# Attention and two MLPs on one core: pairing TensorE's work by width, splitting weights from the decoded tile, and planning the DMAs

## The chip, the cores and the metric

The kernel runs on one core of one Trainium2 chip. The metric is the device time of one execution in microseconds (us). Three runs of the kernel before have a median of 832.0 us (830.35 to 835.03).

## The reference

Inputs and outputs are fp32. Batch 2, 8 heads, 768 positions, head size 64; 16 clusters per head.

```python
mask = argmax(q_n @ c_n) == argmax(k_n @ c_n)      # same cluster
attn = softmax(where(mask, q @ k.T / 8, -1e9)) @ v   # -> x [1536, 512]
h = x @ w_in                                         # 512 -> 2048
x = (h * sigmoid(1.702 * h)) @ w_out                 # 2048 -> 512
out = (silu(x @ w_gate) * (x @ w_val)) @ w_out2      # 512 -> 1536 -> 512
```

The weights of both MLPs arrive in HBM as 64-bit numbers, since setup multiplies them by a 64-bit factor. The kernel decodes them on chip.

## The kernel before, in words

**Attention** comes first (to about 260 us), in an order written out by hand. Beside it the first ten weight items are decoded. The change does not touch this part.

**Precision.** A product of fp32 numbers is made of three TensorE passes over a high and a low part (`product`, L347 on): high by high, high by low, low by high. Each operand is therefore split: `high` is a cast on ScalarE (ACT, L343), `low` a subtraction on VectorE (DVE, L346).

**Decoding.** An item is half of a weight key: 128 partitions by 512 numbers, 512 KB as it arrives ("raw") and 256 KB decoded. The keys are `1`, `2` (first MLP, eight each) and `g`, `v`, `3` (second MLP, six each). `plan_decode` (L940) plans for each item: a DMA of raw into one of three buffers (L242), two ACT operations `small` and `low_bits` (L257, L260), two DVE operations `joined` and `signed` (L263, L268), and a DMA that stores the result in a DRAM scratch (`keep`, L272 on; the second halves of `1`, `g` and `v` take two DMAs). Later `plan_fetch` (L952) reads a whole key back from the scratch (512 KB, L340) into `w`, each time that a batch needs it.

**Units.** The rest is a list of 28 units: for the first MLP two batches of eight, for the second two batches of six. A unit covers 256 hidden columns of 768 rows. Its first stage (`s1`) multiplies x by the unit's weights with moving tiles 384 wide; the trace calls the result `h`. The first batch's units of the first MLP ("classic") have 8 steps of six matmuls; the others use a seven-product scheme (`plan_products`, L1043), once in the first MLP and twice (gate and value) in the second. The activation goes to `c`, is split into `g`, and the second stage (`s2`, the tiles `a` of the trace) multiplies `g` by the split weights `sp` and accumulates in six PSUM banks: `plan_m1_s2` (L1125) for the first MLP in groups of three matmuls, 512 and 256 wide by turns, `plan_m2_s2` (L1191) for the second in groups 512 wide.

**Order.** The loop at the end (L1341 on) goes over the units k = 0 to 27: it plans decodes, splits the second-stage weights of unit k+1, prepares the first-stage weights of unit k+3, and lays the first stage of unit k+2 beside the second stage of unit k: `beside_each_other` (L1291) takes a step of one and a step of the other by turns. This fixes TensorE's order. A decode's ACT operations may not start before the last TensorE task planned when the decode was created (`after`); its raw DMA may.

**The planner.** `Plan.order` (L91) is a list scheduler. It gives each task a latest start, counted back from TensorE's nominal times, then simulates the engines with the tasks' costs and `AFTER` (L64: the time from a task's end to a follower on another engine), and emits each engine's instructions in the order found. On the chip each engine, and SyncE (SP), which issues the DMAs, works in that order. A DMA task occupies SP for 80 ns (160 for a store) in this simulation, and its follower is free 3000 ns later. How many items are decoded, and when, is set by `AHEAD` and `DECODES` (L195): four before the first unit, then five per unit in the classic batch, one per unit in the first MLP's second batch, three per unit after that, in the one order of `items`.

Of the kernel before, what the change touches and what calls it, by code (L numbers as in the profile page):

```python
# [21 lines left out]
class Task:  # L22


    def __init__(self, engine, ns, emit, deps):
        self.engine, self.ns, self.emit, self.deps = engine, ns, emit, set(deps)
        self.end = self.latest = None
# [28 lines left out]
class Plan:  # L56
# [6 lines left out]

    AFTER = {"PE": 230.0, "ACT": 160.0, "DVE": 150.0, "POOL": 120.0, "SP": 3000.0}  # L64

# [25 lines left out]
    def order(self, pe_start, free):  # L91
        for r in self.rings:
            for k, h in enumerate(r.held):
                if h.first is None:
                    continue
                for t in h.users:
                    if k >= r.n:
                        t.deps.update(r.held[k - r.n].users)
                    if k and r.held[k - 1].first is not None:
                        t.deps.add(r.held[k - 1].first)  # L100
        pe = [t for t in self.tasks if t.engine == "PE"]
        for a, b in zip(pe, pe[1:]):
            b.deps.add(a)
        nexts = {t: [] for t in self.tasks}
        left = {t: len(t.deps) for t in self.tasks}
        for t in self.tasks:
            for d in t.deps:
                nexts[d].append(t)
# [9 lines left out]
        def gap(t, s):  # L118
            return 0.0 if t.engine == s.engine == "PE" else self.AFTER[t.engine]

# [9 lines left out]
        left = {t: len(t.deps) for t in self.tasks}  # L130
        ready = {e: [] for e in self.AFTER}
# [5 lines left out]
        while len(done) < len(self.tasks):  # L137
# [31 lines left out]
            for s in nexts[t]:  # L169
                left[s] -= 1  # L170
                if not left[s]:
                    r = max((d.end + gap(d, s) for d in s.deps), default=0.0)
                    ready[s.engine].append((r, s))
# [6 lines left out]
def tile_cluster_attention_two_mlps(ctx: ExitStack, tc: tile.TileContext, qk, v, cen, w1, w2, wg, wv, w3, out):  # L180
# [10 lines left out]
    NB = 512  # L191
    scale = 1.0 / float(D) ** 0.5
    NQK = 5
    RAW, WB, EB, CB, GB, XC, X0 = 3, 3, 2, 4, 4, 7, 4
    DECODES, AHEAD = (5, 1, 3), 4  # L195

# [89 lines left out]

    def new_w():
        return wo_p.tile([128, 512], F32, tag="wo", name="wo")

    def take_in():  # L290

        while True:
            it = items[started[0]]
            fetch_to(started[0] + 1)
            started[0] += 1
            raw = raw_t.pop(it)
            a, t = new_a(), new_t()
            small(a, raw)
            low_bits(t, raw)
            fetch_to(started[0] + 2)  # L300
            joined(t, a)
            yield
            w = new_w()
            signed(w, a, t)
            keep(it, w)
            yield
# [576 lines left out]
    def late(name):  # L883
        if not late_pools:
            att.close()
            xf_p.append(pool(ctx, "xf1", 1))
            xc_p.append(pool(ctx, "xc1", XC - X0))
            xs_p.append(pool(ctx, "xs", 2))
            b_p.extend(pool(ctx, f"b{i}", 1) for i in (1, 2))
            late_pools.update(  # L890
                s=pool(ctx, "s", 1), e=pool(ctx, "e", EB), g=pool(ctx, "g", GB), sp=pool(ctx, "sp", 3),
                a=pool(ctx, "ps_a", 1, space=PSUM),
            )
        return late_pools.get(name)
# [13 lines left out]
    def after_late(make):  # L908
# [6 lines left out]
        "raw": p.ring(RAW, new_raw, [Held(r) for r in raw_t.values()]),  # L915
        "a": p.ring(2, new_a), "t": p.ring(2, new_t), "wo": p.ring(2, new_w),
        "w": p.ring(WB, new_wf, w_held),
# [15 lines left out]
    for i in range(6):  # L933
        rings[f"acc{i}"] = p.ring(1, late_tile("a", [128, 512], F32, f"a{i}"))
    late_rings = ["s", "b1", "b2", "g", "sp", "xs", "xc", "xf", "p1", "u2", "u3"] + [f"acc{i}" for i in range(6)]

    raw_held = dict(zip(raw_t, rings["raw"].held))
    kept = {}

    def plan_decode(it, after=()):  # L940
        raw = raw_held.get(it)
        if raw is None:
            raw = rings["raw"].new()
            p.task("SP", 80, lambda: fetch_into(raw.tile, it), (), [(raw, 0)])
        a, t, w = (rings[n].new() for n in ("a", "t", "wo"))
        p.task("ACT", act(570), lambda: small(a.tile, raw.tile), [(raw, 0)], [(a, 0)], after)
        p.task("ACT", act(560), lambda: low_bits(t.tile, raw.tile), [(raw, 0)], [(t, 0)], after)
        p.task("DVE", dve(512), lambda: joined(t.tile, a.tile), [(a, 0)], [(t, 0)])
        p.task("DVE", dve(512), lambda: signed(w.tile, a.tile, t.tile), [(a, 0), (t, 0)], [(w, 0)])
        kept[it] = p.task("SP", 160, lambda: keep(it, w.tile), [(w, 0)])  # L950

    def plan_fetch(key):  # L952
        w = rings["w"].new()
        p.task("SP", 80, lambda: fetch_w(w.tile, key), (), [(w, 0)], [kept[key + (i,)] for i in range(2) if key + (i,) in kept])
        return w
# [9 lines left out]
    def every(n=None):  # L965
        return (slice(None),) if n is None else (slice(None), slice(*n))

    def plan_classic_blocks(key, early):
        if early:
            out = rings["b0"].held[:2]  # L970
            return out
        w, out = plan_fetch(key), []
        for i in range(2):
            out.append(rings["b0"].new())
            plan_high_low(out[-1], every((0, 2)), lambda i=i: w.tile[:, 2 * i:2 * i + 2], [(w, 0)], 0, 512)
        return out
# [23 lines left out]
    def plan_split(key):  # L1000
        w, out = plan_fetch(key), []
        for i in range(2):
            t = rings["sp"].new()
            plan_high_low(
                t, every(), lambda i=i: w.tile[:, 2 * i:2 * i + 2].rearrange("p a c -> p (a c)"), [(w, 0)], 0, 512
            )
            out.append(t)
        return out
# [17 lines left out]
    def plan_classic(blocks, x, c, by_half):  # L1026
        c += [rings["c"].new() for _ in range(2)]
        for f, t in [(f, t) for t in range(2) for f in range(2)] if by_half else [(f, t) for f in range(2) for t in range(2)]:
            ps = rings[f"m{flip[0]}"].new()
            flip[0] ^= 1  # L1030
            for k in range(2):
                pe_block(ps, 0, blocks[f], k if f == 0 else 1 - k, x[k, t], k == 0, k == 1)
                if k == 0:
# [91 lines left out]
    def plan_m1_s2(gs, sp, acc, first, last):  # L1125
        for f, o in [(f, o) for o in range(KC) for f in range(2)] if last else [(f, o) for f in range(2) for o in range(KC)]:
            m = slice(o * 128, (o + 1) * 128)
            c0 = 256 * (o % 2)
            for a, t0, n, at, opens in (
                (acc[o], 0, NB, slice(0, NB), True),  # L1130
                (acc[4 + o // 2], NB, S - NB, slice(c0, c0 + 256), o % 2 == 0),
            ):
                def emit(a=a, t0=t0, n=n, at=at, opens=opens, f=f, m=m):
                    g, w = gs[f].tile, sp[f].tile
                    product(
                        a.tile[:, at], (w[:, 0, m], w[:, 1, m]), (g[:, 0, t0:t0 + n], g[:, 1, t0:t0 + n]),
                        first and f == 0 and opens, last and f == 1,
                    )
                p.task("PE", 3 * mm(n), emit, [(h, (0, i)) for h in (gs[f], sp[f]) for i in range(2)], [(a, o)])
                yield  # L1140

# [49 lines left out]
    def plan_m2_s2(gs, sp, acc, first, last):  # L1191
        for f, o in [(f, o) for o in range(SC) for f in range(2)] if last else [(f, o) for f in range(2) for o in range(SC)]:
# [7 lines left out]
            p.task("PE", 3 * mm(DM), emit, [(h, (0, i)) for h in (gs[f], sp[f]) for i in range(2)], [(acc[o], 0)])  # L1200
            yield

    def plan_m2_out(b, acc):
        for o in range(SC):
# [13 lines left out]
            p.task("DVE" if o % 2 else "ACT", (dve if o % 2 else act)(DM), emit, [(acc[o], 0)], [(osb, 0)])  # L1218
            p.task("SP", 80, send, [(osb, 0)])

# [16 lines left out]

    def decoded(n=0, upto=None):
        after = [t for t in p.tasks if t.engine == "PE"][-1:]
        while todo and (n > 0 or upto in todo):  # L1240
            plan_decode(todo.pop(0), after)
            n -= 1

    def needs(key):
        if key + (1,) in todo:
            decoded(upto=key + (1,))

    def prepare(u):
        kind, b, q = u
        names = ("1", "gv")[kind == "2"]  # L1250
        if u != units[0]:
            for n in names:
# [5 lines left out]
    def split(u):  # L1258
        kind, b, q = u
        n = {"1": "2", "2": "3"}[kind]  # L1260
        needs((n, q))
        split_of[u] = plan_split((n, q))
# [52 lines left out]

    decoded(AHEAD)
    prepare(units[0])
    prepare(units[1])
    beside_each_other(s1(units[0]), products_of(units[0]), last_values(), SC)
    end_of_pv = [t for t in p.tasks if t.engine == "PE"]  # L1320
# [14 lines left out]
    split(units[0])  # L1335
    decoded(DECODES[0])
    prepare(units[2])
# [73 lines left out]
```

## Time and profile before

| What | Value |
|---|---|
| Median of three runs | 832.0 us (830.35 to 835.03) |
| The profiled execution's own time | 832.42 us |
| Its span in the trace | 830.6 us |
| TensorE busy in the span | 809.4 us (97%) |
| VectorE, ScalarE busy | 637.6 us (77%), 473.6 us (57%) |
| DMA traffic | 103.3 MB, mean 124 GB/s |

In the rows below PE is TensorE's matmuls, PEld its weight loads, DVE VectorE, ACT ScalarE, SP SyncE. "SPq" marks an instruction of SP's sequencer, such as the issue of a DMA. L351 is the line of all matmuls of the MLPs, so the tiles tell them apart. Times are counted from the start of the span.

### The profile page before, as it was taken

The page shows a single profiled execution, that of the slowest core. Times are in us where ns is not written, and L with a number is a line of the kernel's source. Part 1 is how long each engine was busy: PE and PEld are TensorE (multiplying, and loading weights), DVE is VectorE, ACT ScalarE, POOL GpSimd, SP SyncE. Part 2 cuts the span into 40 slices and gives each one's busy share as a digit, 9 for nine tenths or more (in the row PEclk, how much of TensorE's full clock was granted, in tenths as well). Part 3 has the DMA queues.
Part 4 walks back from the last instruction along what each step waited for, and adds up shares of the span by engine and source line. Part 5 has one row for each costly group of instructions (what it writes and reads, how often), then busy time and mean ns, then how long its engine had stood idle before and what let it go on. Part 6 is the DMA issues. An engine that isn't in the chain of part 4 may idle for free.

```text
span 830.6 us, 12798 instructions
## 1 busy us (share of the span) xinstructions
PE 809.4 (97%) x4832; PEld 758.4 (91%) x4832; DVE 637.6 (77%) x1164; ACT 473.6 (57%) x818; POOL 36.4 (4%) x48
## 2 busy tenths in 40 slices
PE   8999999999999999898799999999999999999998
PEld 6999999999999998797689999999999999999996
DVE  7888898898873775567889767988877898877752
ACT  7847767766666765666676446645334554343321
POOL 8530000000000000000000000000000000000000
PEclk9999999999999999999999999999999999999999
DMA  6123123121335687778787432321222112321202
GB/s 129 29 82 88 47 68 89 48 67 50 97 123 202 209 301 271 277 248 296 236 301 236 152 116 89 114 90 64 89 77 77 51 52 102 115 89 51 76 1 77
DMA packets 48710, 103.31 MB, mean 124 GB/s; under 512 B 17044, under 2 KB 22248, under 8 KB 48648
## 3 DMA queue, kind: packets, MB, share of 16 engines
q1 hardware_dynamic: 48568, 102.30, 37.8%
q8 instruction: 38, 0.62, 0.3%
q10 hardware_dynamic: 80, 0.20, 0.1%
q14 instruction: 24, 0.20, 0.1%
HBM read 80.77 MB, written 20.97 MB: 122 GB/s over the span
## 4 chain that ended last, share of the span: by engine, by line
PE 79%; DMA 8%; DVE 7%; ACT 4%; issue 1%; SPq 0%; ACTq 0%; DVEq 0%
PE h L351 30%; PE a L351 21%; PE pv L663 14%; PE st L647 8%; PE smax L600 4%; DMA raw<-in_w 4%; DMA raw<-in_wv 2%; DMA raw<-in_wg 2%; DVE nm L605 1%; PE sims L516 1%; ACT a L257 1%; DVE b L346 1%; DMA w<-scr 1%; DVE t L263 1%; ACT t L260 1%
## 5 line engine op out<-in xcount | busy, mean ns | idle before, releaser
L351 PE MATMUL h<-xc,b 128*128 128x384 f32 x1728 | 350.6, 340 | 12.5 <-ACT c L1038 11.7
L351 PEld LDWEIGHTS h<-xc,b 128*128 128x128 f32 x1728 | 307.6, 189 | 36.4 <-ACT c L1038 16.4
L351 PE MATMUL a<-g,sp 128*128 128x512 f32 (+1 forms) x768 | 157.3, 339 | 0.9 <-DVE xf L1154 0.9
L663 PEld LDWEIGHTS pv<-v,p 128*128 128x128 f32 x1152 | 135.5, 192 | 0.1
L663 PE MATMUL pv<-v,p 128*128 128x65 f32 x1152 | 134.9, 273 | 0.0
L351 PEld LDWEIGHTS a<-g,sp 128*128 128x128 f32 x768 | 122.5, 190 | 10.3 <-DVE xf L1154 1.3
L351 PE MATMUL a<-sp,g 128*128 128x512 f32 x432 | 119.7, 394 | 0.0
L654 ACT ACTIVATE p<-st 128x384 f32<-128x384 f32 x192 | 90.3, 491 | 32.7 <-PE st L647 27.4
L605 DVE TENSOR_REDUCE nm<-smax 128x1 f32<-128x384 f32 x192 | 99.9, 556 | 8.4 <-PE smax L600 7.4
L647 PE MATMUL st<-q,k 128*128 128x384 f32 (+1 forms) x384 | 98.3, 347 | 0.1
L351 PEld LDWEIGHTS a<-sp,g 128*128 128x128 f32 x432 | 79.2, 188 | 7.8
L263 DVE SCALAR_TENSOR_TENSOR t<-a,t 128x512 int32<-128x512 int32 x68 | 46.6, 688 | 50.0 <-ACT t L260 49.8
L343 ACT CAST b<-s 128x512 fp32r<-128x512 f32 x64 | 39.5, 617 | 70.7 <-PE h L351 65.1
L257 ACT ACTIVATE a<-raw 128x512 f32<-128x512 f32 x68 | 45.8, 673 | 57.5 <-DMA raw<-in_w 33.1
L343 ACT CAST b<-w 128x768 fp32r<-128x768 f32 (+1 forms) x48 | 36.5, 763 | 71.8 <-PE h L351 65.4
L647 PEld LDWEIGHTS st<-q,k 128*128 128x128 f32 (+1 forms) x384 | 67.5, 190 | 4.4 <-ACT p L654 2.8
L600 PE MATMUL smax<-k,q 80*128 80x384 f32 x192 | 62.8, 344 | 0.5 <-ACT q L576 0.2
L346 DVE TENSOR_TENSOR g<-c,g 128x768 fp32r<-128x768 f32 x56 | 53.0, 952 | 1.3 <-ACT g L343 1.2
L1060 DVE TENSOR_TENSOR u<-h,p 128x384 f32<-128x384 f32 x64 | 35.6, 556 | 21.5 <-PE h L351 21.4
L346 DVE TENSOR_TENSOR b<-w,b 128x768 fp32r<-128x768 f32 (+1 forms) x48 | 41.5, 866 | 10.9 <-ACT b L343 10.7
L268 DVE SCALAR_TENSOR_TENSOR wo<-a,t 128x512 int32<-128x512 int32 x68 | 46.6, 688 | 2.9 <-DMA scr<-wo 1.5
L343 ACT CAST g<-c 128x768 fp32r<-128x768 f32 x56 | 45.9, 839 | 4.8 <-DVE c L1075 4.8
(118 smaller groups left out, 746.0 us busy)
## 6 DMA issues: line engine op xcount, KB each, us to landing
raw<-in_w SPq DMA_DIRECT2D x44, 512.0 KB, 4.9
w<-scr SPq DMA_DIRECT2D x44, 512.0 KB, 4.2
scr<-wo SPq DMA_DIRECT2D x36, 256.0 KB, 2.5
raw<-in_wg SPq DMA_DIRECT2D x12, 512.0 KB, 3.2
raw<-in_wv SPq DMA_DIRECT2D x12, 512.0 KB
w<-scrg SPq DMA_DIRECT2D x12, 512.0 KB
w<-scrv SPq DMA_DIRECT2D x12, 512.0 KB, 3.2
st<-in_qk SPq DMA_DIRECT2D x15, 384.0 KB, 3.9
```

The lines of the kernel that those rows point to most:

```text
L257: nc.scalar.activation(a, raw[:, :, 1].bitcast(F32), ACTF.Copy, scale=2.0**-112)
L263: nc.vector.scalar_tensor_tensor(out=t, in0=a.bitcast(I32), scalar=3, in1=t, op0=ALU.logical_shift_left, op1=ALU.bitwise_or)
L268: nc.vector.scalar_tensor_tensor(out=w.bitcast(I32), in0=a.bitcast(I32), scalar=-(2**31), in1=t, op0=ALU.bitwise_and, op1=ALU.bitwise_or)
L343: nc.scalar.copy(to, of)
L346: eng.tensor_tensor(out=to, in0=of, in1=hi.bitcast(F32), op=ALU.subtract)
L351: nc.tensor.matmul(out=out_ps, lhsT=lhs[a], rhs=rhs[b], start=(start and j == 0), stop=(stop and j == 2), skip_group_check=True, **kw)
L600: nc.tensor.matmul(out=ps, lhsT=q2(h)[0:ONE + NC, 1, c * 128:(c + 1) * 128], rhs=k2(h)[0:ONE + NC, 1, n * HALF:(n + 1) * HALF],)
L605: nc.vector.tensor_reduce(out=nm_t[h][:, c, n:n + 1], in_=ps, axis=AX.X, op=ALU.max)
L647: nc.tensor.matmul(out=ps, lhsT=k2(h)[0:rows, a, c * 128:(c + 1) * 128], rhs=q2(h)[0:rows, a, at], start=(a == 0), stop=(a == 1),)
L654: nc.scalar.activation(p_t[h, c][:, at], ps, ACTF.Exp, scale=scale)
L663: nc.tensor.matmul(out=pv_t[h][:, i, :], lhsT=p[:, i * 128:(i + 1) * 128], rhs=v_t[h % 3][:, c, :], start=(c == 0 and i == 0), stop=(c == ...
L1060: lambda: nc.vector.tensor_tensor(out=to.tile[:, part], in0=ps.tile[:, 0:HALF], in1=other.tile, op=ALU.add),
```

## The change

Four things are changed together. First, the steps of the first stage are taken two at a time (`by_two`), and the second-stage groups too: two 512-wide groups, then two 256-wide ones in the first MLP, two 512-wide ones in the second. Second, in the first batch the weights of `1` and `2` that are not yet decoded are decoded by the unit that needs them into a tile `wd` (four buffers) and split from there; the store to the scratch stays, for the second batch, and the fetch goes. Third, `g`, `v` and `3` are decoded by a quota for each unit, after that unit's own needs; the decodes ahead of the first unit go. Fourth, the planner gives a raw load or a fetch 2000 ns of SP and a store 1000, has other values in `AFTER`, and treats the order within a ring of buffers as an order of starts (`behind`) and no longer of ends.

```diff
-    AFTER = {"PE": 230.0, "ACT": 160.0, "DVE": 150.0, "POOL": 120.0, "SP": 3000.0}
+    AFTER = {"PE": 210.0, "ACT": 80.0, "DVE": 70.0, "POOL": 120.0, "SP": 2200.0}
...
-                    if k and r.held[k - 1].first is not None:
-                        t.deps.add(r.held[k - 1].first)
+                    if k and r.held[k - 1].first is not None and r.held[k - 1].first not in t.deps:
+                        t.behind.add(r.held[k - 1].first)
...
         def gap(t, s):
-            return 0.0 if t.engine == s.engine == "PE" else self.AFTER[t.engine]
+            if t in s.behind:
+                return -t.ns
+            return 0.0 if t.engine == s.engine != "SP" else self.AFTER[t.engine]
...
-    DECODES, AHEAD = (5, 1, 3), 4
+    DECODES = (1, 1, 1, 2, 2, 4, 4, 4) + (2,) * 8 + (1,) * 3
...
-    def plan_decode(it, after=()):
+    def plan_decode(it, after=(), to="wo"):
...
-            p.task("SP", 80, lambda: fetch_into(raw.tile, it), (), [(raw, 0)])
-        a, t, w = (rings[n].new() for n in ("a", "t", "wo"))
+            p.task("SP", 2000, lambda: fetch_into(raw.tile, it), (), [(raw, 0)])
+        a, t, w = (rings[n].new() for n in ("a", "t", to))
...
-        kept[it] = p.task("SP", 160, lambda: keep(it, w.tile), [(w, 0)])
+        kept[it] = p.task("SP", 1000, lambda: keep(it, w.tile), [(w, 0)])
+        return w
...
+    def plan_pair(key):
+
+        if key + (0,) in kept or key + (0,) not in todo:
+            needs(key)
+            w = plan_fetch(key)
+            return [(w, lambda i=i: w.tile[:, 2 * i:2 * i + 2]) for i in range(2)], key[0] == "1"
+        out = []
+        for i in range(2):
+            todo.remove(key + (i,))
+            w = plan_decode(key + (i,), now(), "wd")
+            out.append((w, lambda w=w: w.tile.rearrange("p (a c) -> p a c", a=2)))
+        return out, False
...
     def plan_split(key):
-        w, out = plan_fetch(key), []
-        for i in range(2):
+        out = []
+        for w, view in plan_pair(key)[0]:
...
-        for f, o in [(f, o) for o in range(KC) for f in range(2)] if last else [(f, o) for f in range(2) for o in range(KC)]:
...
+        order = [(f, o) for o in range(KC) for f in range(2)] if last else [(f, o) for f in range(2) for o in range(KC)]
+        for i in range(0, len(order), 2):
+            for t0, n in acc_parts:
+                for f, o in order[i:i + 2]:
...
+    def decoded(n):
+        for it in [it for it in todo if it[0] in "gv3"][:n]:
+            todo.remove(it)
+            plan_decode(it, now())
...
     def products_of(u):
-        return 8 if classic(u) else 7 if u[0] == "1" else 14
+        return 4 if u[0] == "1" else 7
 
     def groups_of(u):
-        return 16 if u[0] == "1" else 12
+        return 4 if u[0] == "1" else 6
+
+    def by_two(products):
+        for _ in products:
+            next(products, None)
+            yield
...
-    decoded(AHEAD)
...
     for k, u in enumerate(units):
-        decoded(DECODES[0 if classic(u) else 1 if u[0] == "1" else 2])
         if k + 1 < n:
             split(units[k + 1])
         if k + 3 < n:
             prepare(units[k + 3])
+        decoded(DECODES[k] if k < len(DECODES) else 0)
         if k + 1 < n:
             gates(units[k + 1])
         if k + 2 < n:
-            beside_each_other(s1(units[k + 2]), products_of(units[k + 2]), s2(u), groups_of(u))
+            beside_each_other(by_two(s1(units[k + 2])), products_of(units[k + 2]), s2(u), groups_of(u))
```

## Rows read from the trace of the kernel before

**Rows 1.** The page: busy time by engine; GB/s moved in 40 slices of the span.
```profile
PE 809.4 (97%) x4832; PEld 758.4 (91%) x4832; DVE 637.6 (77%) x1164; ACT 473.6 (57%) x818; POOL 36.4 (4%) x48
...
GB/s 129 29 82 88 47 68 89 48 67 50 97 123 202 209 301 271 277 248 296 236 301 236 152 116 89 114 90 64 89 77 77 51 52 102 115 89 51 76 1 77
```

**Rows 2.** Four stretches: us, each engine's busy us (count), granted clock, DMA share, GB/s.
```profile
284.00:443.00 159.00, 145.81 (x795) 132.16 (x793) 114.47 (x180) 105.64 (x188) 0.00 (x0) 0.98 0.80 276
443.00:550.00 107.00, 106.99 (x609) 100.25 (x610) 85.88 (x144) 59.15 (x98) 0.00 (x0) 1.00 0.39 131
550.00:716.00 166.00, 166.00 (x874) 154.96 (x873) 138.40 (x249) 75.57 (x122) 0.00 (x0) 1.00 0.21 70
716.00:831.00 115.00, 110.30 (x557) 100.26 (x556) 75.80 (x134) 40.09 (x67) 0.00 (x0) 1.00 0.19 69
```

**Rows 3.** Waits from 284 to 443 us: who for whom, total us, times, longest.
```profile
ACT a L257 <- DMA raw<-in_w: 29.2, 11, 4.6
PEld h L351 <- ACT c L1038: 16.4, 11, 5.1
PE h L351 <- ACT c L1038: 11.7, 7, 4.6
ACT a L257 <- DMA raw<-in_wg: 9.2, 5, 2.7
```

**Rows 4.** Timeline around the longest wait: start, us, instruction, and idle before it.
```profile
396.96 0.42 SPq L242 DMA_DIRECT2D raw<-in_w  x1
...
403.04 0.66 ACT L257 ACTIVATE a<-raw 128x512 f32<-128x512 f32 x1 [4.57 <-DMA raw<-in_w]
...
403.61 0.48 ACT L1038 ACTIVATE c<-h 128x384 f32<-128x384 f32 x1
...
404.14 1.98 PE L351 MATMUL h<-xc,b 128*128 128x384 f32 x6 [4.65 <-ACT c L1038]
```

**Rows 5.** DMA from 284 to 443 us: total, then issues by line, KB each, us to landing.
```profile
DMA packets 16705, 43.90 MB, mean 276 GB/s; under 512 B 1854, under 2 KB 4670, under 8 KB 16693
...
raw<-in_w SPq DMA_DIRECT2D x24, 512.0 KB, 4.8
w<-scr SPq DMA_DIRECT2D x17, 512.0 KB, 5.9
```

**Rows 6.** Ten-microsecond stretches of the same kind as rows 2.
```profile
290.00:300.00 10.00, 10.00 (x59) 9.38 (x58) 8.78 (x13) 7.21 (x14) 0.00 (x0) 1.00 0.97 316
...
330.00:340.00 10.00, 7.92 (x46) 7.12 (x45) 6.10 (x9) 4.88 (x9) 0.00 (x0) 1.00 0.73 247
...
350.00:360.00 10.00, 10.00 (x50) 9.32 (x49) 5.91 (x9) 5.37 (x10) 0.00 (x0) 0.83 0.74 268
...
400.00:410.00 10.00, 5.86 (x25) 5.45 (x26) 7.38 (x12) 6.33 (x11) 0.00 (x0) 0.83 0.64 233
```

**Rows 7.** The chain that ended last: start, us, what; three stretches.
```profile
295.02 1.06 PE h L351 x6
...
297.13 1.06 PE h L351 x6
...
589.99 2.10 PE h L351 x12
592.09 0.70 PE a L351 x3
592.79 1.06 PE h L351 x6
...
810.14 16.38 PE a L351 x72
```

**Rows 8.** Groups of instructions from 284 to 443 us: count, busy us, mean ns, idle before.
```profile
L257 ACT ACTIVATE a<-raw 128x512 f32<-128x512 f32 x44 | 29.6, 673 | 49.3 <-DMA raw<-in_w 29.2 <-DMA raw<-in_wg 9.2 <-DMA raw<-in_wv 7.0
L263 DVE SCALAR_TENSOR_TENSOR t<-a,t 128x512 int32<-128x512 int32 x43 | 29.4, 688 | 30.2 <-ACT t L260 30.1
...
L343 ACT CAST sp<-w 128x512 fp32r<-128x512 f32 x16 | 10.0, 622 | 0.0
```

More of the change, by code (lines that the diff above doesn't have):

```diff
@@ L25, in __init__ @@
     def __init__(self, engine, ns, emit, deps):
-        self.engine, self.ns, self.emit, self.deps = engine, ns, emit, set(deps)
+        self.engine, self.ns, self.emit, self.deps, self.behind = engine, ns, emit, set(deps), set()
         self.end = self.latest = None
@@ L104, in order @@
         nexts = {t: [] for t in self.tasks}
-        left = {t: len(t.deps) for t in self.tasks}
         for t in self.tasks:
-            for d in t.deps:
+            t.behind -= t.deps
+        left = {t: len(t.deps) + len(t.behind) for t in self.tasks}
+        for t in self.tasks:
+            for d in (*t.deps, *t.behind):
                 nexts[d].append(t)
@@ L129, in order @@
                 t.latest = nominal[t]
-        left = {t: len(t.deps) for t in self.tasks}
+        left = {t: len(t.deps) + len(t.behind) for t in self.tasks}
         ready = {e: [] for e in self.AFTER}
@@ L171, in order @@
                 if not left[s]:
-                    r = max((d.end + gap(d, s) for d in s.deps), default=0.0)
+                    r = max((d.end + gap(d, s) for d in (*s.deps, *s.behind)), default=0.0)
                     ready[s.engine].append((r, s))
@@ L915, in tile_cluster_attention_two_mlps @@
         "raw": p.ring(RAW, new_raw, [Held(r) for r in raw_t.values()]),
[L916 removed]
+        "a": p.ring(2, new_a), "t": p.ring(2, new_t), "wo": p.ring(2, new_wo), "wd": p.ring(WO, late_tile("wd", [128, 512], F32, "wd")),
         "w": p.ring(WB, new_wf, w_held),
@@ L934, in tile_cluster_attention_two_mlps @@
         rings[f"acc{i}"] = p.ring(1, late_tile("a", [128, 512], F32, f"a{i}"))
-    late_rings = ["s", "b1", "b2", "g", "sp", "xs", "xc", "xf", "p1", "u2", "u3"] + [f"acc{i}" for i in range(6)]
+    late_rings = ["s", "wd", "b1", "b2", "g", "sp", "xs", "xc", "xf", "p1", "u2", "u3"] + [f"acc{i}" for i in range(6)]
     raw_held = dict(zip(raw_t, rings["raw"].held))
     kept = {}
-    def plan_decode(it, after=()):
+    def plan_decode(it, after=(), to="wo"):
         raw = raw_held.get(it)
@@ L949, in plan_decode @@
         p.task("DVE", dve(512), lambda: signed(w.tile, a.tile, t.tile), [(a, 0), (t, 0)], [(w, 0)])
-        kept[it] = p.task("SP", 160, lambda: keep(it, w.tile), [(w, 0)])
+        kept[it] = p.task("SP", 1000, lambda: keep(it, w.tile), [(w, 0)])
+        return w
     def plan_fetch(key):
         w = rings["w"].new()
-        p.task("SP", 80, lambda: fetch_w(w.tile, key), (), [(w, 0)], [kept[key + (i,)] for i in range(2) if key + (i,) in kept])
+        p.task("SP", 2000, lambda: fetch_w(w.tile, key), (), [(w, 0)], [kept[key + (i,)] for i in range(2) if key + (i,) in kept])
         return w
@@ L966, in every @@
         return (slice(None),) if n is None else (slice(None), slice(*n))
+    def plan_pair(key):
[9 more added lines that the diff above has]
+        return out, False
     def plan_classic_blocks(key, early):
         if early:
-            out = rings["b0"].held[:2]
-            return out
-        w, out = plan_fetch(key), []
-        for i in range(2):
-            out.append(rings["b0"].new())
-            plan_high_low(out[-1], every((0, 2)), lambda i=i: w.tile[:, 2 * i:2 * i + 2], [(w, 0)], 0, 512)
+            return [(h, (1, 0) if i else (0, 1)) for i, h in enumerate(rings["b0"].held[:2])]
+        of, swapped = plan_pair(key)
+        out = []
+        for i, (w, view) in enumerate(of):
+            b = rings["b0"].new()
+            plan_high_low(b, every((0, 2)), view, [(w, 0)], 0, 512)
+            out.append((b, (1, 0) if swapped and i else (0, 1)))
         return out
@@ L1000, in plan_split @@
     def plan_split(key):
-        w, out = plan_fetch(key), []
-        for i in range(2):
+        out = []
+        for w, view in plan_pair(key)[0]:
             t = rings["sp"].new()
             plan_high_low(
-                t, every(), lambda i=i: w.tile[:, 2 * i:2 * i + 2].rearrange("p a c -> p (a c)"), [(w, 0)], 0, 512
+                t, every(), lambda view=view: view().rearrange("p a c -> p (a c)"), [(w, 0)], 0, 512
             )
@@ L1031, in plan_classic @@
             for k in range(2):
-                pe_block(ps, 0, blocks[f], k if f == 0 else 1 - k, x[k, t], k == 0, k == 1)
+                pe_block(ps, 0, blocks[f][0], blocks[f][1][k], x[k, t], k == 0, k == 1)
                 if k == 0:
@@ L1125, in plan_m1_s2, with emit @@
     def plan_m1_s2(gs, sp, acc, first, last):
-        for f, o in [(f, o) for o in range(KC) for f in range(2)] if last else [(f, o) for f in range(2) for o in range(KC)]:
[L1127 to L1140, printed above, removed]
+        order = [(f, o) for o in range(KC) for f in range(2)] if last else [(f, o) for f in range(2) for o in range(KC)]
+        for i in range(0, len(order), 2):
+            for t0, n in acc_parts:
+                for f, o in order[i:i + 2]:
+                    m = slice(o * 128, (o + 1) * 128)
+                    c0 = 256 * (o % 2) if t0 else 0
+                    a, at, opens = (acc[4 + o // 2], slice(c0, c0 + n), o % 2 == 0) if t0 else (acc[o], slice(0, n), True)
+                    def emit(a=a, t0=t0, n=n, at=at, opens=opens, f=f, m=m):
+                        g, w = gs[f].tile, sp[f].tile
+                        product(
+                            a.tile[:, at], (w[:, 0, m], w[:, 1, m]), (g[:, 0, t0:t0 + n], g[:, 1, t0:t0 + n]),
+                            first and f == 0 and opens, last and f == 1,
+                        )
+                    p.task("PE", 3 * mm(n), emit, [(h, (0, i)) for h in (gs[f], sp[f]) for i in range(2)], [(a, o)])
+            yield
     def plan_m1_out(acc):
@@ L1200, in plan_m2_s2 @@
             p.task("PE", 3 * mm(DM), emit, [(h, (0, i)) for h in (gs[f], sp[f]) for i in range(2)], [(acc[o], 0)])
-            yield
+            if (f if last else o % 2):
+                yield
     def plan_m2_out(b, acc):
@@ L1236, in classic, with now @@
         return u[:2] == ("1", 0)
[L1238 to L1242, printed above, removed]
+    def now():
+        return [t for t in p.tasks if t.engine == "PE"][-1:]
+    def decoded(n):
+        for it in [it for it in todo if it[0] in "gv3"][:n]:
+            todo.remove(it)
+            plan_decode(it, now())
     def needs(key):
-        if key + (1,) in todo:
-            decoded(upto=key + (1,))
+        for i in range(2):
+            if key + (i,) in todo:
+                todo.remove(key + (i,))
+                plan_decode(key + (i,), now())
     def prepare(u):
@@ L1250, in prepare @@
         names = ("1", "gv")[kind == "2"]
-        if u != units[0]:
+        if not classic(u):
             for n in names:
@@ L1314, in last_values @@
             yield
-    decoded(AHEAD)
     prepare(units[0])
     prepare(units[1])
-    beside_each_other(s1(units[0]), products_of(units[0]), last_values(), SC)
+    beside_each_other(by_two(s1(units[0])), products_of(units[0]), last_values(), SC)
     end_of_pv = [t for t in p.tasks if t.engine == "PE"]
```

13 lines of the change are left out of this document (6 added, 7 removed).

## The prediction

> **What bounds the kernel now.** I read the page first. TensorE is busy 809.4 of 830.6 us, and the transfers run near 300 GB/s in the slices from about 290 to 440 us, against some 70 in the last third [rows 1]. So I cut the span by stage [rows 2]. From 443 to 716 us TensorE is never idle at full clock: there only the spacing of its matmuls can be gained. The last stretch is idle 4.7 us, of which the output's way out after the last matmul is about 4; the change leaves that. From 284 to 443 us, the first MLP's first batch and the start of the second, TensorE is busy 145.81 of 159 us: 13.2 us idle, beside 276 GB/s. That is the place.
>
> Who is waited for there? The waits [rows 3] show a ladder: ACT waits for raw (29.2 us in 11 waits for the first MLP's, 9.2 for `wg`'s), and TensorE waits for ACT's activation `c` (11.7 us; its weight loads 16.4). The timeline of the longest one [rows 4] ties them: raw is issued at 396.96; ACT's `small` stands before the activation in its fixed order and starts at 403.04, after 4.57 us idle; the activation comes at 403.61 and TensorE at 404.14, after 4.65 us idle. The engine late is not TensorE's own: a decode whose data had not landed stood ahead of an activation that TensorE needed.
>
> Why is raw late? In that stretch 43.90 MB move, with 4.8 us to landing for raw and 5.9 for a fetch [rows 5]. One decode is 0.524 MB in and 0.262 out, one fetch 0.524. A classic unit plans five decodes and two fetches: 4.98 MB. Its eight rounds of 2.11 us (295.02 to 297.13) [rows 7] take 16.9 us, so it asks for 295 GB/s where 276 are moved. The planner, which charges 80 ns for a load, cannot see that.
>
> **The change, part by part.** The sum starts from the profiled execution, 832.42 us; the median of the three runs, 832.0, stands 0.4 below it, which I neglect.
>
> *Transfers and decodes of the first batch.* Of the 68 items ten are decoded in attention; of the other 58, 22 belong to `1` and `2`. Before, 49 are planned by the end of the classic units (4 + 5 + 8 x 5); after, 22 and a quota of 19, 41. Eleven fetches go (`2` from its second key, `1` from its fifth): 5.8 MB. Of the 44 raw loads in the stretch three go elsewhere: 2.4 MB. 43.75 - 5.8 - 2.4 gives 35.6 MB. At the 276 GB/s of [rows 5] this is 129 us, and TensorE's work without idle takes 159 - 18 = 141. So the transfers no longer pace the batch on average, and the idle time can go. Its size: 13.2 us idle [rows 2]; the clock adds 3.4: the granted share is 0.83 in two stretches of 10 us [rows 6], so 3.4 us in each at 1.2 GHz instead of 2.4, after waits of TensorE, and half of that lost; without those waits the clock should stay up. Restarting costs between nothing and 4.7 us (the weight loads' waits less the matmuls', 16.4 - 11.7 [rows 3]). Ends 16.6 and 21.3; I take **18**, near the low end, since weight loads have slack elsewhere.
>
> What may stay: the quota makes units k = 3 to 6 heavy, six decodes each, and two of these units also fetch: 19.9 MB in 67.5 us of TensorE time, 295 GB/s again. At 276 they need 72.2 us, a lag of 4.7. The quota items are wanted only from unit 16, so a good order lets them slip; but ring order puts them ahead of the next unit's raw. Ends 0 and 4.7; I take **3** to stay, nearer the upper end, as every unit at such a rate shows a wait now.
>
> *Chain of a decoded weight.* A decode may now start only in the unit ahead. Raw 4.8 us [rows 5], two ACT operations of 0.67, two DVE of 0.69, then cast 0.62 [rows 8] and subtraction of about the same: 8.8 us to usable weights, inside the 16.9 of a unit. Nothing on the path, if raw is there; if that cover goes, see the slower rival. The fetch, 5.9 us to landing, and the store before it leave this chain. A new wait comes in: `signed` must find one of the four `wd` tiles free, and DVE's additions queue behind it. A tile is free once it is split, and a first-stage tile is split when a `b0` block is free, about one unit after its decode; four tiles are one unit's need, so I charge 0, and what it would cost is bounded by the unit's own wait in the slower rival. On SP a store waits for `signed`, and the raw loads behind it wait with it, as before; the eleven fetches that go free 11 x 0.4 us of issue there (0.42 for one issue [rows 4]), which is off the path.
>
> *Pairing.* From 550 us a run of six `h` takes 1.06 us, one of twelve 2.10, so the second six take 1.04; three `a` take 0.70 between others but 16.38/72 x 3 = 0.68 in a long run [rows 7]. Each join saves some 0.02 us. A unit of the second MLP has 12 alternations and will have 6; ten such iterations: 10 x 6 x 0.04 = 2.4, or 2.1 by the rounded-off lengths. The first MLP's rounds halve from 8 to 4 in 14 iterations; the 256-wide run has no long row, so it saves 0 to 0.02: 14 x 4 x 0.04 = 2.2. Together **4.3**. Distances between a bank's write, its reading on ACT or DVE and its next use stay: one step and one pair of groups instead of group, step, group. So I charge no new wait.
>
> By the Trainium skill (TensorE: Matmul & The Clock Gate, Back-to-back issue gap), a matmul's gap depends on its own number of columns alone, so the pairing would save nothing. The rows differ: 1.06 against 1.04 for the same six.
>
> *Decodes moved to the second batch.* Units 8 to 15 get 17 decodes in place of 9. Eight more cost DVE 8 x 2 x 0.69 = 11 us over some 122; DVE is busy 85.88 of 107 us there [rows 2], 80%, and becomes about 89%. ACT, at 59.15, has room; so have the transfers, 131 GB/s plus about 50. On the path: 0, if additions to `u` and `c` keep their slack of some 2.5 us; 11 at most. I take 0, since TensorE waits for no one there now.
>
> *The planner's numbers.* DMAs costed at 2000 ns for 0.524 MB are 262 GB/s, close to the 276 moved. `AFTER` for ACT falls from 160 to 80. In [rows 4] the activation ends at 404.09 and TensorE starts at 404.14, 50 ns later, so 80 covers it, with less spare than 160. I price this at 0; its ends are in the rivals.
>
> Sum: 832.4 - 18 - 4.3 + 3 = 813.1, so **813 us**.
>
> **The rivals.** *Transfers still pace the first batch.* For: 233 and 247 GB/s in the stretches with idle [rows 6]. Against: 316 in another, so the low ones are waits too. 35.6 MB at 233 is 153 us, 12 over TensorE's 141, in place of my 3: 822 us (818 to 828).
>
> *Pairing is worth nothing* while the waits go: the 0.02 us at a join might belong to something else than the width, such as the change of tile. Then 832.4 - 18 + 3 = 817 us. For it: only one pair of lengths, 1.06 and 1.04. This is what the Trainium skill's gap rule (TensorE: Matmul & The Clock Gate) would give.
>
> *The new plan does not reorder ACT as meant*: a decode without its data stands ahead of an activation as now, and only pairing is gained: 828 us. DVE at 89% giving back 11 us beside half of the waits ends near there too. For: ACT and SP orders are still fixed in advance. Against: fewer bytes and a cost near the measured rate.
>
> *Slower*: weights reach their unit late. They used to be decoded a unit or more ahead; now raw, decode and split must fit in one unit. If the transfers lag by over one unit (4.7 MB at 276 GB/s), each of eight units waits for raw as long as the longest wait now, 5.1 us [rows 3], and half of them lose 1.7 us of clock after it: 8 x 5.1 + 4 x 1.7 = 47.6, and 832.4 - 18 - 4.3 + 47.6 = 858 us. Against: the lag worked out above is 4.7 us of 16.9.
>
> By the Trainium skill (DMA: Bandwidth & Descriptors, Specifications) a core's HBM limit is about 358 GB/s; by that the lag would be 0 and the sum 810. No stretch of 10 us shown here is above 316.
>
> **How the numbers follow.** Forecast 0.62, with its own range 807 to 818 (18 and 3 at their ends, the pairing between 2 and 4.3). Transfers pace it 0.14. Pairing worth nothing 0.06. Not reordered 0.10. Weights late 0.08. A measurement of this kernel can tell about 0.5% from no change, 4 us: faster is below 828, 0.62 + 0.14 + 0.06 = 0.82; same 0.10; slower 0.08. The range takes the first three, 0.82: 807 to 828 us.
>
> **What would show it.** Right: from 284 us on TensorE's idle before `c` of L1038 falls from 11.7 us to under 4, the granted clock stays at 1.0 from 20 us on, fetches `w<-scr` drop by 11, runs of twelve `h` and six `a` take 2.10 and about 1.38 us, and the total of transfers falls from 103.3 MB to about 97.5. The end of the classic batch should come some 17 us earlier. Wrong: idle of TensorE before DVE's `u` or `c` after 440 us (the moved decodes), before `sp` or `b` (late weights), or ACT still idle before `a<-raw` with an activation behind it.

## The result, and the profile after

The changed kernel takes 812.0 us, the median of four runs (811.68 to 812.05). The kernel before took 833.5 beside it. The ratio is 0.9742, with a 95% interval of 0.9702 to 0.9782, so it is 2.6% faster. The profiled execution took 812.05 us, 20.4 less than that of before; its span is 810.1 us.

The page of the changed kernel (busy time; GB/s in 40 slices; total of the DMA packets), to be held against [rows 1]:
```profile
PE 802.2 (99%) x4832; PEld 753.2 (93%) x4832; DVE 635.8 (78%) x1164; ACT 476.7 (59%) x818; POOL 36.3 (4%) x48
...
GB/s 129 29 88 74 64 69 51 72 86 16 54 202 154 27 174 260 233 260 281 247 259 226 231 158 183 153 99 85 72 72 79 78 53 77 131 78 54 77 1 78
DMA packets 47125, 97.54 MB, mean 120 GB/s; under 512 B 16868, under 2 KB 22072, under 8 KB 47064
```

The same four stages, cut where the work of [rows 2] now lies (columns as there):
```profile
284.00:426.00 142.00, 142.00 (x812) 132.82 (x811) 113.82 (x178) 104.18 (x182) 0.00 (x0) 1.00 0.75 245
426.00:533.00 107.00, 106.73 (x612) 99.80 (x611) 91.78 (x154) 67.15 (x110) 0.00 (x0) 1.00 0.57 189
533.00:697.00 164.00, 163.96 (x864) 151.52 (x863) 138.26 (x249) 76.99 (x124) 0.00 (x0) 1.00 0.22 74
697.00:811.00 114.00, 108.81 (x551) 98.05 (x549) 74.73 (x133) 40.33 (x66) 0.00 (x0) 0.99 0.19 68
```
Nearly all of the gain lies in the first row. TensorE is busy for all of its 142 us, and it runs 812 matmuls there, where before 795 took 159 us. The granted clock is 1.00; it was 0.98. At 245 GB/s the 142 us hold 34.8 MB, where the 159 us before held 43.9.

Who waited for whom from 284 to 424 us on ACT of the changed kernel (columns as in [rows 3]):
```profile
ACT c L1057 <- PE h L355: 20.7, 17, 3.7
...
ACT a L261 <- DMA raw<-in_w: 2.7, 2, 2.1
```
The ladder has turned round. ACT's wait for raw of the first MLP is 2.7 us in two waits, not 29.2 in eleven; and the activation `c` waits for TensorE instead of TensorE for it.

The chain of the changed kernel (start, us, what), in the first and in the second MLP, to be held against [rows 7]:
```profile
286.00 2.11 PE h L355 x12
288.11 2.09 PE a L355 x12
...
302.81 2.11 PE h L355 x12
...
582.33 4.34 PE h L355 x24
586.66 1.39 PE a L355 x6
588.05 2.08 PE h L355 x12
...
605.42 4.36 PE h L355 x24
```
The pairs are there: twelve `h`, then six `a` in 1.39 us. But once per unit of the second MLP 24 `h` follow each other, and they take 4.34 or 4.36 us, not the 4.16 of two runs of twelve. A unit of gate and value, the stretch from one such run to the next, is 605.42 - 582.33 = 23.09 us long; before it was 2 x 11.60 = 23.20.

### The profile page after: what moved, and what is told of

It reads as the page before. It is cut to its first block, busy times and chain, and to the rows that moved or that the text cites. A ratio compares the mean times of both kernels' runs of the same rounds, so it can differ in the third digit from the quotient of the medians.

```text
span 810.1 us, 12760 instructions
## 1 busy us (share of the span) xinstructions
PE 802.2 (99%) x4832; PEld 753.2 (93%) x4832; DVE 635.8 (78%) x1164; ACT 476.7 (59%) x818; POOL 36.3 (4%) x48
## 4 chain that ended last, share of the span: by engine, by line
PE 92%; DVE 5%; ACT 2%; issue 1%; ACTq 0%; DVEq 0%
PE h L355 36%; PE a L355 27%; PE pv L667 14%; PE st L651 8%; PE smax L604 4%; DVE nm L609 1%; PE sims L520 1%; PE xt L696 1%; DVE xc L350 0%; PE warm L440 0%; ACT g L347 0%; DVE wo L272 0%; ACT xc L347 0%; DVE t L267 0%; DVE xs L327 0%
## 5 line engine op out<-in xcount | busy, mean ns | idle before, releaser
L355 PE MATMUL h<-xc,b 128*128 128x384 f32 x1728 | 326.0, 337 | 0.6 <-ACT p L1100 0.5
L355 PEld LDWEIGHTS h<-xc,b 128*128 128x128 f32 x1728 | 300.0, 188 | 9.4 <-DVE u L1079 2.2
L355 PE MATMUL a<-g,sp 128*128 128x512 f32 (+1 forms) x768 | 144.3, 336 | 0.0
L355 PEld LDWEIGHTS a<-g,sp 128*128 128x128 f32 x768 | 124.9, 188 | 16.9
L355 PE MATMUL a<-sp,g 128*128 128x512 f32 x432 | 109.6, 393 | 0.0
L355 PEld LDWEIGHTS a<-sp,g 128*128 128x128 f32 x432 | 80.2, 188 | 13.2
L347 ACT CAST b<-w 128x768 fp32r<-128x768 f32 (+1 forms) x40 | 31.6, 792 | 44.9 <-PE h L355 35.9
L267 DVE SCALAR_TENSOR_TENSOR t<-a,t 128x512 int32<-128x512 int32 x68 | 46.6, 687 | 13.2 <-ACT t L264 12.9
L350 DVE TENSOR_TENSOR b<-w,b 128x768 fp32r<-128x768 f32 (+1 forms) x40 | 35.9, 900 | 24.6 <-ACT b L347 24.5
L347 ACT CAST g<-c 128x768 fp32r<-128x768 f32 x56 | 45.2, 834 | 10.6 <-DVE c L1094 10.3
L350 DVE TENSOR_TENSOR b<-s,b 128x512 fp32r<-128x512 f32 x64 | 44.0, 687 | 2.0 <-ACT b L347 0.4
```

Source lines behind the costliest of these rows:

```text
L267: nc.vector.scalar_tensor_tensor(out=t, in0=a.bitcast(I32), scalar=3, in1=t, op0=ALU.logical_shift_left, op1=ALU.bitwise_or)
L347: nc.scalar.copy(to, of)
L350: eng.tensor_tensor(out=to, in0=of, in1=hi.bitcast(F32), op=ALU.subtract)
L355: nc.tensor.matmul(out=out_ps, lhsT=lhs[a], rhs=rhs[b], start=(start and j == 0), stop=(stop and j == 2), skip_group_check=True, **kw)
```

## The experiments

Four things were changed at once, so I first took them apart: pairing, planner, and what I call traffic (direct split and quotas). All times are medians. The kernel before was run with each set: 833.6, 834.1, 834.5 and 833.7 us.

**Pairing alone**, on the kernel before:
```diff
+            if (f if last else o % 2):
+                yield
...
+            beside_each_other(by_two(s1(units[k + 2])), products_of(units[k + 2]), s2(u), groups_of(u))
```


> The kernel before with the pairing alone. If pairing saves at the joins only, as the shorter rounds of the changed kernel show (a unit of the second MLP 23.09 us in place of 23.20, a classic one 16.80 in place of 16.88), some 2 us go and the first batch keeps its idle time: 828 to 832 us. By the prediction's 4.3 us it would be 828 to 829. Rival: the joins are worth nothing: 832 to 834. Rival: pairing also loosens the order around ACT, so that the waits for raw no longer reach TensorE: below 825, with less than 6 us of matmul idle before the activation c.

829.5 us, ratio 0.9956 (0.9943 to 0.997). That is 4.1 us, with 2.5 to 4.8 by the interval. TensorE's waits from 284 us on come to 13.0 us, as many as before, so what is gained is not idle time but the joins:
```profile
PE h L351 <- ACT c L1038: 7.9, 6, 3.0
PE h L351 <- ACT p L1081: 2.0, 2, 1.8
PE h L351 <- DVE c L1060: 1.9, 1, 1.9
PE h L351 <- DVE b L346: 1.2, 1, 1.2
```
My 4.3 fits this kernel. Runs of 24 stand in it too, and here they take no longer than two runs of twelve:
```profile
603.07 4.17 PE h L351 x24
...
626.00 4.17 PE h L351 x24
```
A unit of gate and value takes 626.00 - 603.07 = 22.93 us, where it took 23.20: 2.7 us in the ten.

**No pairing**, on the changed kernel, the old alternation of single steps put back.

> The changed kernel with the old alternation of single steps. If pairing is worth 2 us at the joins: 813.5 to 815. By the prediction's 4.3: 816. If it is worth nothing: 812. If it carried part of the removal of the waits: above 818, with idle before c from 284 to 426 us.

812.5 us (812.51 to 813.07), 0.5 above the changed kernel. So in the changed kernel the pairing is worth 0.5, of the 2 to 4.3 expected, and since the two ran in different sets even that is not clear of nothing. TensorE waits for no engine from 284 us on here; the small waits in the runs of 24 come with the pairing. But they do not come with it alone, as the kernel before with pairing showed. The order of DVE differs. In the changed kernel an addition to `c` stands ahead of the one that reads `h` and frees its bank, and a weight load of TensorE waits for that one:
```profile
607.38 0.55 DVE L1094 TENSOR_TENSOR c<-u,c 128x384 f32<-128x384 f32 x1
607.85 0.55 DVE L1079 TENSOR_TENSOR u<-h,p 128x384 f32<-128x384 f32 x1
...
608.45 1.01 PEld L355 LDWEIGHTS h<-xc,b 128*128 128x128 f32 x6 [0.22 <-DVE u L1079]
```
In the kernel before with pairing alone they stand the other way round:
```profile
605.26 0.56 DVE L1060 TENSOR_TENSOR u<-h,p 128x384 f32<-128x384 f32 x1 [0.28 <-PE h L351]
605.73 0.55 DVE L1075 TENSOR_TENSOR c<-u,c 128x384 f32<-128x384 f32 x1
```
So the new planner's order and the runs of 24 cost this time together; the run with the old planner, two further on, bears it out. Which of the planner's edits turned the two round was not tested.

**The planner alone**, on the kernel before (`AFTER`, `behind`, the DMA costs).

> The kernel before with the new planner alone (AFTER, starts in ring order, DMA costs). Theory that the transfers' amount paces the first batch: 43.75 MB at 276 GB/s stay 159 us whatever the order, so at most a few us go: 825 to 832. Rival that the order was at fault and not the amount: the waits before c go without one byte less: 814 to 818, with matmul idle from 284 us on under 3 us.

812.5 us, ratio 0.975 (0.9731 to 0.9769): below even the rival's 814 to 818, and nearly the whole gain, with all 103.3 MB still moved. The stretch of the batch in that kernel (columns as in [rows 2]):
```profile
284.00:424.00 140.00, 140.00 (x799) 131.50 (x798) 105.80 (x163) 97.71 (x171) 0.00 (x0) 1.00 0.78 259
```
TensorE is never idle, with no fetch removed. The total of the data was not what set the time. But the stretch itself moves less: 259 GB/s over 140 us are 36.3 MB for 799 matmuls, where 43.9 MB went beside 795 before. The planner has moved decodes out of the batch, and so to about the 35.6 MB that I forecast for it.

**The old planner**, on the changed kernel.

> The changed kernel with the old planner (AFTER, ring order of ends, 80 and 160 ns for DMAs). Theory that the amount paces the batch: 9 MB less suffice, most of the waits stay away: 812 to 818. Rival that the order was at fault: the waits come back: 822 to 831, with ACT idle before a<-raw and TensorE idle before c. If both are needed: 818 to 824.

815.4 us (813.5 to 818.7), ratio 0.9795 (0.9762 to 0.9829). Direct split and quotas, with the pairing, also suffice, nearly. ACT still waits for raw (10.3 us in 7 waits for the first MLP's), but no such wait reaches TensorE; what does are single waits of 1.4 us or less for `c`, `u` and `p`. So the traffic part and the planner each remove nearly all of the idle time by itself. What follows is only that neither is necessary. The longest wait of TensorE from 284 us on, and ACT's for raw:
```profile
PE h L351 <- DVE c L1075: 1.4, 1, 1.4
...
ACT a L257 <- DMA raw<-in_w: 10.3, 7, 2.7
```
The runs of 24 of the changed kernel take 4.17 to 4.20 us in the second MLP here, so it is the new planner that lengthens them:
```profile
585.34 4.17 PE h L351 x24
608.27 4.20 PE h L351 x24
```

**Traffic alone**: as before, and without the pairing.

> The changed kernel with the old planner and without the pairing, that is the direct split and the quotas alone. With the pairing this was 815.4. If the lower traffic needs neither: 815 to 818, about the 815.4 of the run with pairing. If pairing had loosened the order there: above 819.

819.1 us (818.14 to 820.08), ratio 0.9821 (0.9795 to 0.9847). This is just above the 815 to 818 that I expected if the traffic part needed nothing else. Beside the old planner the pairing is worth 3.7 us by the medians of two sets (819.1 to 815.4) and 2.2 by their ratios, whose intervals overlap; the 4.1 on the kernel before is the firmer number.

**The DMA costs alone**, on the kernel before. The planner has several new numbers; this kernel changes its DMA costs alone (a fetch like a raw load, an output like a store):
```diff
-    AFTER = {"PE": 230.0, "ACT": 160.0, "DVE": 150.0, "POOL": 120.0, "SP": 3000.0}
+    AFTER = {"PE": 230.0, "ACT": 160.0, "DVE": 150.0, "POOL": 120.0, "SP": 2200.0}
-            p.task("SP", 80, lambda: fetch_into(raw.tile, it), (), [(raw, 0)])
+            p.task("SP", 2000, lambda: fetch_into(raw.tile, it), (), [(raw, 0)])
...
-        kept[it] = p.task("SP", 160, lambda: keep(it, w.tile), [(w, 0)])
+        kept[it] = p.task("SP", 1000, lambda: keep(it, w.tile), [(w, 0)])
```


> The kernel before with the DMA costs alone (2000 and 1000 ns of SP, 2200 to a follower); gaps between engines and ring order as before. If the planner's blindness for transfer time made the bad order of ACT: 812 to 816, no idle of TensorE before c. Rival that the gaps or the ring order did it: 825 to 834. If each does a part: 817 to 824.

813.9 us (813.81 to 815.01), ratio 0.9762 (0.9737 to 0.9786). These costs bring all but some 2 us of the whole change.

**The planner's other edits alone**, with DMAs at 80 and 160 ns.

> The kernel before with the planner's other edits alone (AFTER of PE, ACT and DVE, no gap within an engine, ring order of starts); a DMA still costs 80 or 160 ns of SP and 3000 to a follower. Theory of the DMA costs: 826 to 836, the waits for raw as before. Rival: the ring order of ends held decodes back, and this alone gives 812 to 817.

830.9 us, ratio 0.9953 (0.9932 to 0.9973). TensorE still waits 7.1 us for `c`. The costs are the planner's part that counts.

How do they help? The issues from 284 to 424 us (KB each, median us to landing), first of the kernel before:
```profile
raw<-in_w SPq DMA_DIRECT2D x23, 512.0 KB, 4.8
...
raw<-in_wg SPq DMA_DIRECT2D x8, 512.0 KB, 3.2
raw<-in_wv SPq DMA_DIRECT2D x8, 512.0 KB
```
Then of the kernel with the DMA costs:
```profile
raw<-in_w SPq DMA_DIRECT2D x19, 512.0 KB, 4.8
...
raw<-in_wg SPq DMA_DIRECT2D x6, 512.0 KB
raw<-in_wv SPq DMA_DIRECT2D x6, 512.0 KB, 3.3
```
31 raw loads in place of 39, in the same 140 us, though TensorE gets further in them. The decodes that nobody needs yet slip into later units, and the stretch moves 33.1 MB (236 GB/s):
```profile
284.00:424.00 140.00, 140.00 (x798) 131.45 (x798) 101.60 (x156) 92.07 (x161) 0.00 (x0) 1.00 0.71 236
```
And ACT's order has room for the ones that are late, as its waits in that kernel show:
```profile
ACT c L1038 <- PE h L351: 28.1, 20, 2.6
...
ACT a L257 <- DMA raw<-in_w: 4.8, 4, 1.4
```

**Half the costs**: 1000 and 500 ns, otherwise the same edit.

> The kernel before with half the DMA costs: 1000 ns for 0.524 MB (524 GB/s), 500 for a store, 2200 to a follower. A classic unit then costs SP 5 x 1.5 + 2 x 1 = 9.5 us of 16.9, where the full costs ask for 5 x 3 + 2 x 2 = 19. Theory that the full costs help because they exceed the unit's time and so push decodes into later units: half of them bind nowhere, and the waits stay: 826 to 834. Rival that any cost on SP, or the shorter way to a follower, gives ACT a better order: 812 to 818.

826.8 us, ratio 0.9908 (0.9882 to 0.9935), with 38 raw loads (22, 8 and 8) in the same stretch. First the row that holds as many matmuls as those above, then the waits from 284 to 430 us:
```profile
284.00:438.00 154.00, 144.38 (x800) 132.01 (x799) 115.34 (x181) 106.08 (x188) 0.00 (x0) 0.99 0.83 276
```
```profile
ACT a L257 <- DMA raw<-in_w: 24.1, 12, 4.6
...
PE h L351 <- ACT c L1038: 6.9, 5, 2.5
```
The same 2200 ns to a follower, the same lines, but half the cost: most of the gain is gone, and the batch moves 42.5 MB (276 GB/s over 154 us). By the plan's own sum a classic unit now costs SP 9.5 us of its 16.9, with the full costs 19; this fits an occupancy that pushes decodes out only once it exceeds what a unit has. It does not prove it, for one number sets three things in these kernels: how long SP is occupied, when the plan believes that data has landed (80 + 3000 ns after the start of the load before, 2000 + 2200 with the full costs, 1000 + 2200 with half; raw takes 4.8 us), and, by the old ring order, the least distance of two raw loads, which is the same sum. The whole planner has dropped that distance and the idle time is gone there too, so it is not needed. Occupancy and belief were not taken apart: 80 ns with a follower at some 4100 was not run.

**Twice the costs**: 4000 and 2000 ns.

> The kernel before with twice the DMA costs: 4000 ns for 0.524 MB (131 GB/s), 2000 for a store. The 22 decodes and some 17 fetches that the first batch must have cost SP 22 x 6 + 17 x 4 = 200 us then, more than the 141 of its matmuls, so the plan believes TensorE late and misplaces other work. Theory that the cost must lie near the rate moved (276 GB/s): 818 to 840. Rival that any cost large enough to hold the decodes back will do: 812 to 816, and then the value need not be measured.

931.6 us, ratio 1.1184 (1.1159 to 1.1209): far worse than either side expected. The first batch in that kernel (as [rows 2]), and what TensorE waited for from 260 us on (as [rows 3]):
```profile
284.00:424.00 140.00, 119.74 (x614) 106.76 (x614) 65.15 (x94) 63.00 (x109) 0.00 (x0) 0.93 0.43 148
```
```profile
PE h L351 <- ACT b L343: 53.3, 20, 7.0
PE h L351 <- DVE b L346: 12.1, 19, 1.3
```
The plan made its own belief true: the transfers run at 148 GB/s where 276 were moved before, and TensorE waits for first-stage weights `b`. Of the three costs tried, only the one near the rate that the chip moves serves: 2000 ns for 0.524 MB, 262 GB/s.

**No direct split**, on the changed kernel; quotas, planner and pairing stay:
```diff
-        if key + (0,) in kept or key + (0,) not in todo:
+        if True:
```


> The changed kernel with every weight fetched from the scratch in place of the direct split; quotas, planner and pairing stay. With the planner that knows the transfers, eleven fetches more (5.8 MB) only move: 811.5 to 813.5. Rival, my prediction's reading that the amount sets the time: a chain longer by store and fetch, some 10 us in one unit of 16.9, and heavier units 3 to 6: 816 to 826, with idle of TensorE before sp or b.

831.0 us (828.0 to 835.0), ratio 0.9968 (0.9944 to 0.9992). Here I had expected no loss, and the rival was right, beyond its number. The waits from 284 to 424 us:
```profile
PEld h L355 <- DVE b L350: 6.6, 7, 1.8
PEld h L355 <- ACT b L347: 6.2, 6, 2.1
PE h L355 <- ACT b L347: 4.6, 5, 1.8
PE h L355 <- DVE b L350: 4.2, 5, 1.5
...
ACT b L347 <- DMA w<-scr: 3.6, 4, 2.6
```
TensorE waits for `b`, not for `c`: weights come late. With the new schedule a weight of the first batch is decoded in the unit ahead of its use, and store, fetch and split do not fit in behind it. The direct split is what makes that schedule possible.

**Runs of two**, on the changed kernel. The second MLP's twelve groups are laid in seven steps and the last two units of the first MLP in eight:
```diff
-            if (f if last else o % 2):
+            at += 1
+            if at in (2, 4, 6, 7, 8, 10, 12):
                 yield
```


> The changed kernel with the second MLP's twelve groups laid out in seven steps (2, 2, 2, 1, 1, 2, 2) and the last two units of the first MLP in eight, so that no four first-stage steps follow each other. Theory: the pairing's gain at the joins, 3.7 us by the spacing of matmuls, was given back where four steps stand in a row and the third or fourth waits for its bank to be read (4.36 us for 24 matmuls, not 4.16); without such runs 809 to 810.5. Rival: it was lost in the spacing itself or elsewhere: 811.5 to 812.5, with runs of 24 gone all the same.

810.5 us (809.66 to 810.88), ratio 0.9716 (0.9692 to 0.9741), 1.5 below the changed kernel's 812.0; it was run in another set, with the kernel before at 834.1 in place of 833.5. The chain in the second MLP:
```profile
565.80 2.08 PE h L355 x12
567.88 0.70 PE a L355 x3
568.58 2.10 PE h L355 x12
570.68 0.70 PE a L355 x3
...
588.77 2.08 PE h L355 x12
```
No run of 24 is left, and a unit takes 588.77 - 565.80 = 22.97 us, where it took 23.09 and, before, 23.20.

**Planner and runs of two without the rest**: the kernel before with the new planner and that pairing, no direct split, no quotas.

> The kernel before with the new planner and the pairing in runs of two, without the direct split and the quotas. If those two bring nothing once the planner knows the transfers: 810 to 811.5, the same as the changed kernel with runs of two (810.5). If they still save waits: 812 to 816.

809.4 us (809.25 to 810.66), ratio 0.9704 (0.9672 to 0.9736). It lies below the kernel before and, in another set, 2.6 us below the changed kernel, moves all the bytes of before, and has half of the change in it. Its only wait of TensorE on another engine from 284 us on is 0.3 us.

## Why the prediction was right, and where it was not

The time, 813 forecast and 812.0 measured, came out of a sum in which two errors cancelled, and that is luck: 3 us that did not stay, and nearly 4 of the pairing that did not come.

*The place and the size of the gain: right.* Idle time, clock and restarts in the first batch were put at 18 us, with ends of 16.6 and 21.3. From 284 us on, 17 us are gone for the first stretch and 17 more matmuls are done in it, some 3 us of work (142 us for 812): 20, of which under a half is pairing. Four paired rounds take 302.81 - 286.00 = 16.81 us, eight single ones took 311.88 - 295.02 = 16.86 (295.02 stands in [rows 7]):
```profile
311.88 1.08 PE h L351 x6
```
That leaves over 19. The signs listed for "right" are there: no idle before `c`, the clock at 1.00 up to 697 us, 33 fetches in place of 44, 97.5 MB, the batch some 20 us earlier. One listed for "wrong" is there in small: weight loads wait 2.2 us in all for DVE's `u`, in the runs of 24.

*The reason given for it: wrong in what brings it about, open in the rest.* The step that failed is the price of 0 for "the planner's numbers", and with it the whole 18 us put on the removed fetches and the quota. The new planner alone takes the idle away with all 103.3 MB moved (812.5), and its DMA costs nearly so (813.9). The traffic part, alone, gives 819.1, and beside planner and runs of two it gives nothing (810.5 with it, 809.4 without). It was nearly sufficient and not needed.

What stays open is "the transfers no longer pace the batch on average". In every kernel here that lost the idle time, some 800 matmuls of the batch go beside 33 to 36 MB; those in which ACT still stands long at raw ahead of `c` have 42 to 45. No run has the larger amount in the batch without the idle time, so fewer bytes there and a better order of ACT were not separated. The 276 GB/s that I divided by is not all that the chip moves, though. With the planner's other edits alone 60 us ran at 325, the DMA share at 0.95, and still with 5.4 us idle:
```profile
288.00:348.00 60.00, 54.56 (x299) 50.15 (x298) 43.29 (x65) 41.03 (x74) 0.00 (x0) 0.97 0.95 325
```

*The 3 us that would stay: wrong.* It came of dividing by 276 GB/s, which made units 3 to 6 lag by up to 4.7 us. TensorE has no wait there.

*Pairing, 4.3: right in the joins, wrong in "I charge no new wait".* Alone it gives 4.1; in the changed kernel 0.5. I had compared a bank's distances for pair beside pair, and missed that seven pairs beside six leave two pairs in a row. There the third and fourth step reuse a bank with one step between, in which DVE's addition or ACT's copy must fit. In the order of the old planner they do (4.17 us for 24), in that of the new one they do not (4.34 to 4.36): I priced the pairing and the planner apart. Without those runs the pairing brings 2.0 (812.5 to 810.5) or, with the schedule of before, 3.1 (812.5 to 809.4). The mis-sized term is the first MLP's: I gave it 2.2, and a unit of the first batch went from 16.86 to 16.81 us, 0.7 in 14 units if all save alike; the second MLP's is as forecast where nothing waits, 10 x (23.20 - 22.97) = 2.3.

*Decodes moved to the second batch: right.* DVE is busy 91.78 of 107 us there, 86% (89 forecast), and TensorE idles 0.27.

*The slower rival* did not come, but its mechanism did where the direct split was taken out (831.0), and with doubled costs (931.6). The chain of 8.8 us inside a unit of 16.9 was judged rightly, but it leaves no room for a store and a fetch as well. I noted that these leave the chain and gave that no price.

*Pairing worth nothing* is refuted by the first run: 2.5 to 4.8 us from the order of widths and tiles, with as much idle time as before. Twelve `h` take 2.08 us in the second MLP and 2.11 in the first, with the same 384 columns. The formula of the Trainium skill (TensorE: Matmul & The Clock Gate, Back-to-back issue gap) has a matmul's own columns alone in it. The section gives it for a matmul by itself and says that in a stream the weight load counts too; the weight loads are alike here (128x128), so this does not make the difference.

## What to carry to other kernels

Where a static order puts a waiting instruction ahead of one that the bound engine needs, look at what the planner believes before cutting work: a transfer's cost in the plan, set to the rate that the trace shows, did here what the direct split and the quotas did, and half or double of it did not. A high transfer rate beside idle time does not show that transfers are the limit, and a run with the same total does not show that they are not: compare the bytes that go beside the same work. When steps are paired, count the places where the two sides do not divide evenly, for two pairs in a row halve the time in which a bank must be read, and look there at the order of the engine that reads it.

## What was not expected of the hardware

The stage that moved 276 GB/s beside 13.2 us of idle TensorE runs without any at 236 (33.1 MB in 140 us, with the DMA costs alone) and at 259 (the whole planner). Raw takes 4.8 us to landing at 276 and at 236 alike, so the lower rate did not make the single load faster. The spacing of equal matmuls depends on their neighbours by some 0.02 us at a join, which is small, but there were enough joins for 3 to 4 us (829.5 against 833.6).
